# Moving the second pair of state copies of a chunked recurrence from VectorE to ScalarE

## The chip, the cores and the metric

The kernel runs on one core of a Trainium2 chip. A core has a matrix engine (TensorE, in the profile PE, with its weight loads as PEld), VectorE (DVE), ScalarE (ACT), GpSimd (POOL) and a queue for transfers (SyncE, SP). Each works through its own list of instructions in order, and they wait for one another by semaphores. The metric is the device time of one execution in microseconds (us); lower is better.

## The reference

The computation has two stages. The first is a linear recurrence over 768 steps with a 40 x 40 state for each of 4 x 8 = 32 heads. The second is a small mixture of four attention experts on its result.

```python
for t in range(S):                                   # 768 steps, 32 heads, D = 40
    y[:, :, t] = np.einsum('bhd,bhde->bhe', rt, state)
    Sa = np.einsum('bhde,bhe->bhd', state, at)
    state_decay = state * wt[:, :, None, :] - np.einsum('bhd,bhe->bhde', Sa, bt)
    state = state_decay + np.einsum('bhd,bhe->bhde', vt, kt)
x = y of all heads side by side                      # 4 x 768 x 320
for e in range(4):                                   # causal attention of each expert, top 2 of 4 mixed
    a = softmax(causal(scale * (x @ wq[e]) @ (x @ wk[e]).T))
    out += (mask of the top 2) * gate[e] * (a @ (x @ wv[e]) @ wo[e])
```

The change lies in the first stage alone.

## The kernel before

**How the recurrence is tiled.** The 768 steps are cut into 24 chunks of 32 steps, and four chunks make a window (six windows). Within a chunk the steps are written as matrix products: the decays are folded into scaled copies of k, b and a, a triangular 32 x 32 system for each head and chunk is inverted, and the chunk's outputs and the next state come out of a few products. The 32 heads go in four groups of eight, and one group in one chunk is a *unit*: 96 units, numbered `u = 4 * chunk + group`.

**The seven parts of a unit.** `unit(u)` gives them by letters:

- `k` (L358): PE turns the scaled keys (L361); ScalarE copies them into `LS`, rows 0 to 63 (L365).
- `g` (L366): PE multiplies with the group's matrix `GL` (L371); ScalarE copies the result into `GT` (L372).
- `u` (L373): PE applies the inverted system `TT` (L377); ScalarE writes the result into `R` (L378).
- `v` (L379): PE turns `R` (L383); ScalarE copies it into `VU` (L384).
- `f` (L385): PE multiplies with `RB` (L388); VectorE masks the result into `R` (L389).
- `y` (L390): PE multiplies `LS` with `R` into `py` (L396), which holds the output and the new state. The state goes into the next chunk's `R1` (in the profile also `R`) by ScalarE (L406), or in the last chunk of a window, with a factor, by VectorE (L404). The output goes into `XT` by VectorE (L408).
- `t` (L415): PE turns the new state of two units, sixteen heads (L420), into the one tile `PT`, and two copies put it into the next chunk's `LS`, rows 64 to 103. These two copies are the lines of the change. `t` runs for every second unit: for group 0 (heads 0 to 15) and for group 2 (heads 16 to 31), so twice a chunk and 23 times each. In the kernel before, the pair of group 0 is ScalarE's (L427) and the pair of group 2 VectorE's (L425).

**The order.** The order of instructions is written out by hand. The main loop (L511) goes through steps `n`, and in each through the parts in the order of `MAIN` (L433), each for a unit some steps back:

`u` of unit n-1, `g` of n, `y` of n-3, `f` of n-2, `t` of n-6 (even n only), `k`, `v` of n-1.

So between the turnings of `t` in step n and the product `y` that reads their copies PE has `v` of step n, `u` and `g` of step n+1. For group 2, `t` falls on steps with n divisible by 4, for group 0 two steps before.

**The side work.** Into the slots behind these parts the tables `SIDE`, `SIDE1`, `SIDE2` put the preparation of the next window: `prep` (two scans on VectorE at L267 and L273, products at L276 and L281 on VectorE or GpSimd, flags `JK` on ScalarE at L264, copies on ScalarE at L283, the 32 matmuls of `m` and `n` at L289 with VectorE's mask at L290), and `invert` (chains of products and sums at L319 and L321 on VectorE and GpSimd). The sixth window has nothing to prepare, and in its place the second stage's weights are made ready. Side work stands in the same queues as the units' parts, in the order in which it was written.

**The PSUM ring.** `u`, `g`, `f`, `k`, `v`, `m` and `n` share four PSUM buffers `ps`; `PT` has one buffer, and `py` two.

Of the kernel before, what the change touches and what calls it, by code (L numbers as in the profile page):

```python
# [8 lines left out]
AF = mybir.ActivationFunctionType  # L9
# [132 lines left out]
def recurrence(tc, ctx, I, xT, FL, CM, early, tail=None, KP=(11, 11, 11, 11, 11, 11)):  # L142
# [5 lines left out]
    V, A, T, PL = nc.vector, nc.scalar, nc.tensor, nc.gpsimd  # L148

    def ps(shape):  # L150
        return pp.tile(shape, F32, name="ps", tag="ps", bufs=4)
# [198 lines left out]
    def unit(u):  # L350
        c, g = divmod(u, 4)
        w, cw = divmod(c, 4)
        i = w * NG + g
        h0 = 8 * g
        gl, tt, ls, r1, r2, rb, sc = GF[w % 2], TF[w % 2], LS[c % 2], R1[c % 2], R2[c % 2], RB[c % 2], SC[i % 12]
        gt, vu, xt, py = GT[g], VU[u % 2], XT[g // 2][:, 4 * (g % 2):4 * (g % 2) + 4], PY[u % 2]
        rn, ln = R1[(c + 1) % 2], LS[(c + 1) % 2]
        def s_k():  # L358
            p_k = ps([128, 4, 128])
            for p in range(4):  # L360
                T.transpose(p_k[:, p, 0:104], KB[i % NKB][0:104, p * 4 + cw:p * 4 + cw + 2, :].rearrange("q c k -> q (c k)"),  # L361
                            ident[0:104, 0:104])
            p_k = p_k.rearrange("q p (s e) -> q (p s) e", s=2)[:, :, 0:40]
            for k in range(2):
                A.activation((ls, ln)[k][0:64, h0:h0 + 8], p_k[64 * k:64 * k + 64], AF.Copy)  # L365
        def s_g():  # L366
            p_g = ps([33, 8, 40])
            for h in range(8):
                o = 1024 * g + 64 * ((h // 2) * 4 + cw) + 32 * (h % 2)
                r = 104 * ((h0 + h) // 2) + 64 * (h % 2)  # L370
                T.matmul(p_g[:, h], gl[:, o:o + 33], r1[:, r:r + 40], start=True, stop=True)  # L371
            A.activation(gt[32 * g:32 * g + 32], p_g[0:32], AF.Copy)  # L372
        def s_u():  # L373
            p_u = ps([33, 8, 40])
            for h in range(8):
                o = 64 * ((h // 2) * 4 + cw) + 32 * (h % 2)
                T.matmul(p_u[:, h], tt[:, o:o + 33], gt[:, h, :], start=True, stop=True)  # L377
            A.activation(hd(r2[32:64, 40 * h0:40 * h0 + 320], 40), p_u[0:32], AF.Copy, scale=-1.0)  # L378
        def s_v():  # L379
            p_t = ps([80, 4, 66])  # L380
            for p in range(4):
                o = 40 * (h0 + 2 * p)
                T.transpose(p_t[:, p], r2[0:66, o:o + 80], ident[0:66, 0:66])  # L383
            A.activation(vu[0:80], p_t[:, :, 0:64], AF.Copy)  # L384
        def s_f():  # L385
            p_f = ps([64, 8, 32])
            for p in range(4):
                T.matmul(p_f[:, 2 * p:2 * p + 2], vu[:, p, :], rb[:, 4 * g + p, :], start=True, stop=True)  # L388
            V.tensor_tensor(hd(r2[0:64, 1280 + 32 * h0:1536 + 32 * h0], 32), p_f, mask[:, None, :].to_broadcast([64, 8, 32]), op=OP.mult)  # L389
        def s_y():  # L390
            a = r2[:, 0:40]
            for p in range(4):
                for s in range(2):
                    h = h0 + 2 * p + s
                    m = bass.AP(a.tensor, a.offset + 40 * h, [a.ap[0], [1280 - 8 * h, 2], [1, 40]])
                    T.matmul(py[64 * s:64 * s + 40, p], ls[:, h, :], m, start=True, stop=True, tile_position=(0, 64 * s))  # L396
            for s in range(2):
                q = slice(64 * s, 64 * s + 40)
                if c < 23:
                    o = rn[64:104, 52 * h0:52 * h0 + 416].rearrange("q (p e) -> q p e", p=4)[:, :, 64 * s:64 * s + 40]  # L400
                    st = py[q, :, 0]
                    if cw == 3:
                        pn = PC[((c + 1) // 4 * NG + g) % 12]
                        V.tensor_tensor(o, st, pn[q, :, None].to_broadcast([40, 4, 40]), op=OP.mult)  # L404
                    else:
                        A.activation(o, st, AF.Copy)  # L406
            def decay():
                V.tensor_tensor(xt[:, :, 32 * cw:32 * cw + 32], py[0:104, :, 1, 0:32],  # L408
                                sc.rearrange("q (p c) t -> q p c t", p=4)[:, :, cw, 0:32], op=OP.mult)
                if cw == 3:  # L410
                    for s in range(2):
                        nc.sync.dma_start(xT.rearrange("b (p s e) t -> b s e p t", s=2, e=40)[g, s, :, :, 128 * w:128 * w + 128],
                                          xt[64 * s:64 * s + 40])
            return decay
        def s_t():  # L415
            if c == 23:
                return
            for P in range(8):
                o = 52 * h0 + 104 * P
                T.transpose(PT[0:104, P // 4, 104 * (P % 4):104 * (P % 4) + 104], rn[0:104, o:o + 104], ident[0:104, 0:104])  # L420
            for s in range(2):
                o = ln[64:104, h0 + s:h0 + 16:2].rearrange("q (b p) e -> q b p e", b=2)
                x = PT[64 * s:64 * s + 40, :, 0:416].rearrange("q b (p e) -> q b p e", p=4)[:, :, :, 64:104]
                if g:
                    V.tensor_copy(o, x)  # L425
                else:
                    A.activation(o, x, AF.Copy)  # L427
        return dict(k=s_k, g=s_g, u=s_u, v=s_v, f=s_f, y=s_y, t=s_t)


# [80 lines left out]
    for n in range(NU + 4):  # L511
# [4 lines left out]
        for s, (x, d) in enumerate(MAIN):  # L516
            if x == "k":
                g = {7: 0, 1: 1, 3: 2, 5: 3}.get(n % 8)
# [440 lines left out]
```

## Time and profile before

| what | value |
|---|---|
| time, median of 3 runs | 735.41 us (730.02 to 738.67) |
| the profiled execution | 737.55 us, its span 735.5 us |
| PE / PEld / VectorE / ScalarE / GpSimd busy | 636.8 / 563.0 / 519.7 / 466.6 / 333.5 us |
| mean granted clock of TensorE | 0.919 |
| first and last copy of L425 | 112.4 to 480.2 us |
| L425 | 46 copies, 490 ns each at the median |
| L427 | 46 copies, 430 ns each at the median |

The recurrence's steps fill about 80 to 482 us of the span, the second stage the rest. A row of waits says who stood still, on which line, until which other engine's instruction had ended: total, number of times, longest. In the timeline a row is a run of like instructions with its start, its length and, in brackets, the idle time just before it and what ended that. In windows a row is a stretch with the busy time of each engine, the clock that TensorE was granted, the busy share of the DMA engines and what they moved.

### The profile page before, as it was taken

The page shows a single profiled execution, that of the slowest core. Times are in us where ns is not written, and L with a number is a line of the kernel's source. Part 1 is how long each engine was busy: PE and PEld are TensorE (multiplying, and loading weights), DVE is VectorE, ACT ScalarE, POOL GpSimd, SP SyncE. Part 2 cuts the span into 40 slices and gives each one's busy share as a digit, 9 for nine tenths or more (in the row PEclk, how much of TensorE's full clock was granted, in tenths as well). Part 3 has the DMA queues.
Part 4 walks back from the last instruction along what each step waited for, and adds up shares of the span by engine and source line. Part 5 has one row for each costly group of instructions (what it writes and reads, how often), then busy time and mean ns, then how long its engine had stood idle before and what let it go on. Part 6 is the DMA issues. An engine that isn't in the chain of part 4 may idle for free.

```text
span 735.5 us, 22110 instructions
## 1 busy us (share of the span) xinstructions
PE 636.8 (87%) x8801; PEld 563.0 (77%) x8801; DVE 519.7 (71%) x1270; ACT 466.6 (63%) x1144; POOL 333.5 (45%) x512
## 2 busy tenths in 40 slices
PE   5531798898899888988899999979989999999996
PEld 4531788897789777987798999978868777887774
DVE  8899879668866876677657435258797687658651
ACT  6695487477657755766566768727656565656752
POOL 5475388139704850486018301013565354433641
PEclk8555799999999989989999999999999999999999
DMA  7851653575357535753452382143123113201101
GB/s 201 201 149 37 133 159 107 121 199 137 97 136 190 129 89 124 199 130 96 112 147 70 96 227 72 34 140 98 44 69 96 36 39 86 62 28 45 37 32 45
DMA packets 88551, 78.13 MB, mean 106 GB/s; under 512 B 54776, under 2 KB 72952, under 8 KB 88440
## 3 DMA queue, kind: packets, MB, share of 16 engines
q1 hardware_dynamic: 88296, 76.54, 39.9%
q8 instruction: 71, 1.16, 0.7%
q14 instruction: 40, 0.33, 0.2%
q10 hardware_dynamic: 144, 0.10, 0.1%
HBM read 56.17 MB, written 14.16 MB: 96 GB/s over the span
## 4 chain that ended last, share of the span: by engine, by line
PE 59%; DVE 22%; ACT 8%; issue 3%; DMA 1%; SPq 0%; POOL 0%; ACTq 0%; DVEq 0%; POOLq 0%
PE py L396 7%; PE ps L377 6%; PE ot L843 5%; PE ps L289 5%; PE ps L371 5%; PE ps L388 5%; PE sc L795 4%; PE pt L420 4%; PE pt L825 3%; PE pt L852 3%; PE pt L717 3%; PE ps L361 3%; PE pt L736 3%; DVE SC L273 2%; DVE MT L321 2%
## 5 line engine op out<-in xcount | busy, mean ns | idle before, releaser
L817 POOL TENSOR_TENSOR P<-P,m 128x128 f32<-128x128 f32 (+2 forms) x96 | 87.6, 934 | 103.1 <-DVE m L813 50.3
L396 PE MATMUL py<-R,LS 128*40 128x80 f32 x1536 | 84.9, 244 | 31.2 <-DVE LS L425 28.8
L289 PE MATMUL ps<-AB,KB 104*64 104x64 f32 x768 | 68.4, 262 | 38.6 <-ACT LS L365 16.1
L321 POOL TENSOR_TENSOR MT<-MT,TP 128x84 f32<-128x84 f32 (+13 forms) x169 | 89.9, 532 | 13.2
L289 PEld LDWEIGHTS ps<-AB,KB 104*64 104x64 f32 x768 | 63.3, 174 | 42.5 <-ACT LS L365 16.3
L389 DVE TENSOR_TENSOR R<-ps,CM 64x256 f32<-64x256 f32 x96 | 39.9, 415 | 78.4 <-PE ps L388 77.3
L396 PEld LDWEIGHTS py<-R,LS 128*40 128x40 f32 x1536 | 63.7, 122 | 36.3 <-DVE LS L425 33.8
L806 ACT ACTIVATE P<-sc,m 128x128 f32<-128x128 f32 (+2 forms) x96 | 60.7, 633 | 30.2 <-DVE m L805 24.5
L805 DVE TENSOR_REDUCE m<-sc 128x1 f32<-128x128 f32 (+2 forms) x96 | 59.4, 622 | 27.9 <-PE sc L798 26.8
L377 PE MATMUL ps<-GT,TT 128*33 128x40 f32 x1536 | 76.1, 207 | 0.0
L406 ACT ACTIVATE R<-py 40x160 f32<-40x160 f32 x144 | 42.5, 295 | 46.0 <-PE py L396 42.3
L377 PEld LDWEIGHTS ps<-GT,TT 128*33 128x33 f32 x1536 | 65.0, 116 | 7.5 <-issue 1.0
L795 PE MATMUL sc<-ks,qs 128*128 128x384 f32 (+4 forms) x256 | 64.4, 353 | 3.9 <-ACT P L806 3.6
L388 PE MATMUL ps<-RB,VU 128*64 128x64 f32 x768 | 63.4, 228 | 2.1 <-ACT VU L384 2.1
L365 ACT ACTIVATE LS<-ps 64x320 f32<-64x320 f32 x96 | 41.4, 431 | 30.6 <-PE ps L361 29.4
L388 PEld LDWEIGHTS ps<-RB,VU 128*64 128x64 f32 x768 | 56.1, 144 | 3.5 <-ACT VU L384 3.5
L825 PE MATMUL pt<-CM,P 128*128 128x128 f32 x336 | 51.9, 276 | 2.1 <-ACT pt L831 1.7
L319 POOL TENSOR_TENSOR TP<-LT,MT 128x220 f32<-128x220 f32 (+9 forms) x100 | 49.7, 497 | 7.8
L384 ACT ACTIVATE VU<-ps 80x256 f32<-80x256 f32 x96 | 36.4, 379 | 26.3 <-PE ps L383 24.5
L372 ACT ACTIVATE GT<-ps 32x320 f32<-32x320 f32 x96 | 40.7, 424 | 14.8 <-PE ps L371 11.4
L795 PEld LDWEIGHTS sc<-ks,qs 128*128 128x128 f32 x256 | 41.3, 191 | 11.2 <-ACT P L806 8.5
L378 ACT ACTIVATE R<-ps 32x320 f32<-32x320 f32 x96 | 40.9, 426 | 7.6 <-PE ps L377 5.6
(148 smaller groups left out, 1498.0 us busy)
## 6 DMA issues: line engine op xcount, KB each, us to landing
RB<-in_RB SPq DMA_DIRECT2D x24, 320.0 KB
EK<-in_EK SPq DMA_DIRECT2D x18, 416.0 KB
ks<-ks SPq DMA_DIRECT2D x32, 192.0 KB
R<-in_VG SPq DMA_DIRECT2D x24, 208.0 KB
EW<-in_EA SPq DMA_DIRECT2D x18, 214.5 KB
R<-in_VT SPq DMA_DIRECT2D x48, 80.0 KB
R<-in_RT SPq DMA_DIRECT2D x24, 160.0 KB
xT<-XT SPq DMA_DIRECT2D x48, 80.0 KB
```

Source lines behind the costliest of these rows:

```text
L289: T.matmul(p_a[:, p, cc, :], kb[0:104, n, :], AB[0:104, n, :], start=True, stop=True)
L319: return [lambda: e.tensor_tensor(tmp, row[:, None, :].to_broadcast([128, m, n]), M[:, r0:r0 + m, j][:, :, None].to_broadcast([128, m, n]) ...
L321: lambda: e.tensor_tensor(o, o, tmp, op=OP.add)]
L377: T.matmul(p_u[:, h], tt[:, o:o + 33], gt[:, h, :], start=True, stop=True)
L388: T.matmul(p_f[:, 2 * p:2 * p + 2], vu[:, p, :], rb[:, 4 * g + p, :], start=True, stop=True)
L396: T.matmul(py[64 * s:64 * s + 40, p], ls[:, h, :], m, start=True, stop=True, tile_position=(0, 64 * s))
L406: A.activation(o, st, AF.Copy)
L795: T.matmul(ps[:, c, 0:cw], QS[b][:, e, o], KS[b][:, e, z, k], start=(z == 0), stop=(z == 1 and not last), skip_group_check=True)
L805: V.tensor_reduce(m[:, 0, t:t + 1], ps[:, 0:ch, 0:cw], axis=AX.XY, op=OP.max, negate=True)
L806: later(DE, lambda: A.activation(pv, ps[:, 0:ch, 0:cw], AF.Exp, bias=m[:, 0, t:t + 1], accum_out=m[:, 1, t:t + 1]))
L817: PL.tensor_tensor(P[:, 0:n], P[:, 0:n], m[:, 3, t:t + 1].to_broadcast([128, n]), op=OP.mult)
L825: T.transpose(p[:, 128 * y:128 * y + 128], st["P"][t][:, 128 * c:128 * c + 128], ident)
```

## The change

The branch on the group falls away, and both pairs of copies are ScalarE's. The same data go from the same place to the same place, as before; the line numbers behind it fall by three, so that the copies of both groups now stand on L424.

```diff
             for s in range(2):
                 o = ln[64:104, h0 + s:h0 + 16:2].rearrange("q (b p) e -> q b p e", b=2)
                 x = PT[64 * s:64 * s + 40, :, 0:416].rearrange("q b (p e) -> q b p e", p=4)[:, :, :, 64:104]
-                if g:
-                    V.tensor_copy(o, x)
-                else:
-                    A.activation(o, x, AF.Copy)
+                A.activation(o, x, AF.Copy)
         return dict(k=s_k, g=s_g, u=s_u, v=s_v, f=s_f, y=s_y, t=s_t)
```

The instructions of VectorE around the ninth of its 23 pairs, in the third window (`SC` is the scan's result, `AB` the scaled a, `TP` and `MT` the inversion; - stands before and not now):

```order
 L273 SCALAR_TENSOR_TENSOR SC_97<-EW_83,D1P_86 104x528
 L276 TENSOR_TENSOR AB_112<-EA_84,SC_97 40x16x32
-L425 COPY LS_123<-pt 40x8x40 x2
 L319 TENSOR_TENSOR TP_119<-MT_117 128x99
 L321 TENSOR_TENSOR MT_117<-MT_117,TP_119 128x9x11
```

The pair stood behind a scan and a product of the preparation; it goes, and nothing else moves.

The instructions of ScalarE at the same place (`VU`, `GT` and `R` are the unit's own tiles, `JK` the flag; + stands now and not before):

```order
 L372 ACTIVATE GT_134<-ps 32x320
 L406 ACTIVATE R_124<-py_79 40x4x40 x2
+L424 ACTIVATE LS_123<-pt 40x8x40 x2
 L384 ACTIVATE VU_129<-ps 80x256
 L264 ACTIVATE JK,FL<-EW_83,CM 104x512
```

The pair now stands between the copies of `y` and the copy of `v`, the place that the pair of group 0 has two steps earlier. PE, GpSimd and the transfer queue keep their instructions and their order.

## The prediction

> **What bounds the kernel now.** I read the page first, then the waits of the stretch in which the edited line runs, then that line's own rows, the timeline around one copy, and the windows between copies. Busy times show no engine that is full:
>
> ```profile
> span 735.5 us, 22110 instructions
> PE 636.8 (87%) x8801; PEld 563.0 (77%) x8801; DVE 519.7 (71%) x1270; ACT 466.6 (63%) x1144; POOL 333.5 (45%) x512
> ```
>
> So the recurrence is set by who waits for whom. The view of waits between 100 and 482 us has (total us, times, longest us):
>
> ```profile
> DVE R L389 <- PE ps L388: 74.8, 57, 2.8
> ACT R L406 <- PE py L396: 40.3, 16, 4.4
> PE py L396 <- DVE LS L425: 28.8, 25, 3.2
> ACT LS L427 <- PE pt L420: 14.1, 19, 1.2
> PE ps L371 <- ACT VU L384: 2.2, 3, 1.1
> PE ps L388 <- ACT VU L384: 1.6, 7, 0.3
> ```
>
> Of what PE waits for, 28.8 us is for VectorE's copy at L425, and no row names L427, ScalarE's copy of the same shape, as a thing waited for. The two take (ns, least/median/most):
>
> ```profile
> L425 DVE COPY LS<-pt x46: 483/490/496, 112.4 to 480.2; 40x320 f32<-40x320 f32 x46
> L427 ACT ACTIVATE LS<-pt x46: 428/430/433, 102.8 to 474.7; 40x320 f32<-40x320 f32 x46
> ```
>
> The timeline around the ninth of the 23 VectorE pairs shows why PE waits (start us, length us; in brackets the idle time before it):
>
> ```profile
> 253.76 0.92 PE L420 MATMUL pt<-CM,R 104*104 104x104 f32 x8
> ...
> 256.46 0.41 ACT L372 ACTIVATE GT<-ps 32x320 f32<-32x320 f32 x1
> 256.81 1.25 DVE L273 TENSOR_TENSOR_SCAN SC<-EW,D1P 104x528 f32<-104x528 f32 x1
> 258.09 0.75 DVE L276 TENSOR_TENSOR AB<-EA,SC 40x512 f32<-40x512 f32 x1
> 258.87 1.01 DVE L425 COPY LS<-pt 40x320 f32<-40x320 f32 x2
> 259.41 1.68 PE L396 MATMUL py<-R,LS 128*40 128x80 f32 x15 [3.23 <-DVE LS L425]
> ...
> 261.26 0.62 ACT L406 ACTIVATE R<-py 40x160 f32<-40x160 f32 x2 [4.40 <-PE py L396]
> ...
> 261.86 0.42 DVE L389 TENSOR_TENSOR R<-ps,CM 64x256 f32<-64x256 f32 x1 [1.04 <-PE ps L388]
> ```
>
> The turnings that the pair reads end at 253.76 + 0.92 = 254.7, but the copies start at 258.87, behind VectorE's preparation of the next window (a scan of 1.25, a product of 0.75). PE stands 3.23 us before L396, and ScalarE 4.40 us behind PE. The bound here is not a busy engine but a short copy in a long queue.
>
> **The change part by part.** I cut the trace at the starts of VectorE's pairs; the first row holds one pair, the 35.60, 38.10 and 37.80 rows two each, the last eight (stretch; length, busy time and count of PE, weight loads, DVE, ACT, POOL; granted clock, DMA share, GB/s):
>
> ```profile
> 112.40:129.90 17.50, 15.08 (x264) 13.84 (x264) 15.84 (x38) 11.40 (x30) 15.30 (x29) 0.90 0.36 100
> 129.90:152.70 22.80, 21.65 (x360) 20.25 (x360) 14.75 (x36) 13.27 (x30) 2.25 (x6) 0.93 0.61 136
> 167.70:203.30 35.60, 28.46 (x528) 26.04 (x528) 31.32 (x65) 23.18 (x62) 29.25 (x53) 0.95 0.41 110
> 203.30:224.20 20.90, 20.29 (x344) 19.07 (x344) 13.77 (x34) 12.75 (x29) 0.00 (x0) 0.92 0.59 136
> 224.20:240.20 16.00, 15.18 (x315) 14.35 (x313) 11.32 (x25) 11.90 (x29) 9.19 (x14) 1.00 0.77 204
> 240.20:278.30 38.10, 30.95 (x528) 28.30 (x528) 30.52 (x66) 23.18 (x62) 27.55 (x51) 0.87 0.39 107
> 278.30:299.20 20.90, 20.32 (x344) 19.09 (x344) 13.51 (x32) 12.75 (x29) 0.00 (x0) 0.92 0.60 131
> 315.60:353.40 37.80, 31.27 (x528) 28.87 (x528) 29.52 (x66) 23.29 (x62) 26.73 (x49) 0.86 0.36 98
> 353.40:373.20 19.80, 19.19 (x327) 18.04 (x328) 11.05 (x29) 11.12 (x25) 0.00 (x0) 0.91 0.52 117
> 389.90:480.00 90.10, 88.34 (x1796) 83.29 (x1796) 41.83 (x114) 64.81 (x169) 23.02 (x56) 1.00 0.37 99
> ```
>
> PE's wait for L425 in these stretches, in the same order without the 224.20 one, which has none:
>
> ```profile
> PE py L396 <- DVE LS L425: 1.7, 2, 1.5
> PE py L396 <- DVE LS L425: 2.2, 2, 2.0
> PE py L396 <- DVE LS L425: 4.1, 4, 2.4
> PE py L396 <- DVE LS L425: 2.8, 1, 2.8
> PE py L396 <- DVE LS L425: 4.8, 3, 3.2
> PE py L396 <- DVE LS L425: 2.8, 1, 2.8
> PE py L396 <- DVE LS L425: 5.0, 4, 2.9
> PE py L396 <- DVE LS L425: 2.8, 1, 2.8
> PE py L396 <- DVE LS L425: 2.0, 5, 0.9
> ```
>
> They sum to 28.2 us. Removed from VectorE: 46 copies of 0.49, a pair 1.01 as the timeline has it, 23.2 us in all. Added to ScalarE: 46 of 0.43, 19.8 us in all, each pair in the place that the matching pair of L427 has two steps earlier. There ScalarE's copies already cost PE no wait, so I count PE's wait for this copy as gone: **28.2 us**, the first term.
>
> What is late next. At the ninth pair VectorE would have finished its last job ahead of L389 1.01 us sooner, and it idled 1.04 us before L389, so L389 can come 2.05 us earlier at once, not 3.23. The rest has to come out of VectorE's idle time in the following steps. For the seven pairs of the 17.50, 35.60, 38.10 and 37.80 rows VectorE's idle time is 1.66 + 4.28 + 7.58 + 8.28 = 21.8, and the removed pairs add 7.1; neighbours on VectorE stand 0.03 us apart (256.81 + 1.25 to 258.09), about 1 us in a stretch of 32 instructions, 7 in all, which cannot be had. That caps these seven at 22 us. Their waits are 15.6, so the cap lies above the first term, but not far. In the four stretches with the matmuls of the next window (22.80, 20.90 twice, 19.80) VectorE idles 7 to 9 us and PE is busy 19 to 22, so their waits, 10.6, come back whole.
>
> A second gain is possible on top. The stretches that open with a wait show a granted clock of 0.86 to 0.95, the 16.00 one without a wait 1.00. Length times (1 - clock) over the eight low rows is 1.75 + 1.60 + 1.78 + 1.67 + 4.95 + 1.67 + 5.29 + 1.78 = 20.5 us of PE time at full clock. If the waits cause the low clock, the first seven pairs reach their cap of 22, the four others 10.6 + 6.7 = 17.3, and with the last row's 2.0 the gain is 41: the upper end. [...]
>
> The lower end is what VectorE is relieved of where it is late: 13 pairs are waited for over 0.5 us (one in each of the first two rows, two in each long row, one in each of the three that follow these, two in the last), 13 x 1.01 = 13 us. Between 13 and 41 I take 28.2, the waits themselves, the only row that is a measured wait of the engine that sets the pace; it stands in the middle.
>
> The new wait. ScalarE runs in order: behind the pair stand VU (L384), in some steps the flag JK (L264), then R (L378), GT (L372) and L406; PE's next turnings wait for R, its next products for GT and VU. At the ninth pair ScalarE would start it at 254.7, end the rest 0.89 later than now, at 256.87 + 0.89 = 257.8, and still idle over 3 us of the 4.40 if L396 did not move. When L396 moves up to 259.41 - 3.23 = 256.2, right behind the matmuls before it, ScalarE is about 1 us late for L406, and part of the gain passes through it. That is inside my caps. For the ten pairs that PE does not wait for by over 0.5 us, the price is between 0 and 10 x 0.89 = 8.9 us; in the last row PE is busy 88.34 of 90.10 and ScalarE 64.81, which its eight pairs raise to 72, so I take **1 us**.
>
> [...]
>
> The sum: the profiled execution took 737.55, its span of 735.5 and 2.05 around it. 737.55 - 28.2 + 1 = 710.4. The median of the runs shown, 735.41, lies 2.1 lower, which gives 708.2. I say 709.
>
> **The rivals.**
>
> *VectorE's queue was the bound, and the copy only showed it.* PE runs ahead and then waits for R from L389, which stands behind the same scans. Then a waited pair brings only 1.01 us: 737.55 - 13 + 1 = 725.5. For it: in the 35.60 row VectorE is busy 31.32. Against: L389 itself waits for PE 74.8 us, in 57 places. 12%. In its extreme form PE's wait just changes its name and the time stays at 737: 8%.
>
> *The clock comes back too.* 737.55 - 41 = 696.5. For it: low clock only behind waits. Against: the last row has waits and a clock of 1.00, so not every wait lowers it. 12%. [...]
>
> *ScalarE becomes the bound, and the kernel is slower.* If each pair's 0.89 us lands on the path through VU, R and GT, 23 x 0.89 = 20.5 are added, and PE's 28.2 reappear as waits on ScalarE: 737.55 + 20.5 = 758. It decides where ScalarE's idle time in a step falls under 0.89 us. For it: PE already waits for VU in ten places, 3.8 us in all, and ScalarE's 40.3 us before L406 exist only because PE is late. Against: in the 38.10 row ScalarE is busy 23.18, and its two pairs more, 1.8 us, still fit. 8%.
>
> **How the numbers follow.** Forecast 60% (702 to 718), VectorE's queue 12% (725), name change 8% (737), clock 12% (697), ScalarE 8% (758). From 697 to 727 the forecast, the first rival and more than half of the clock's are held, 8 in 10. About 1% is what a measurement of this kernel can tell from no change, 728 and 743 here. Faster: 60 + 12 + 9 = 81%; same: 8 and a part of the 725 case, 11%; slower 8%.
>
> **What would show it.** Right: no wait of PE for the copy; PE's other waits up by less than 5 us; ScalarE's idle time before L406 down from 40.3 to under 20; the plain stretches at 15.5 to 17.5 us each instead of 17.5 to 19; the granted clock above 0.95 between 112 and 373 if the clock follows. Wrong: a new row of 10 us or more in which PE waits for R of L389 (VectorE's queue) or for VU, R or GT (ScalarE), or longer stretches in the last 90 us.

## The result and the profile after

The changed kernel takes 703.12 us (median of 4 runs, 702.29 to 706.51), the kernel before beside it 736.95 (4 runs). The ratio is 0.957, with a 95% interval of 0.949 to 0.964; forecast were 709 us and a range of 697 to 727. A second set of runs gave 706.13 against 735.55, ratio 0.960 (0.955 to 0.965). The profiled execution took 706.51, 31.0 less than the one before.

The page of the changed kernel, span and busy times:

```profile
span 704.4 us, 22098 instructions
PE 618.0 (88%) x8801; PEld 547.4 (78%) x8801; DVE 496.1 (70%) x1224; ACT 486.4 (69%) x1190; POOL 342.6 (49%) x512
```

VectorE has lost 23.6 us of work and ScalarE gained 19.8, about what the 46 copies take on each. PE is busy 18.8 us less with the same 8801 matmuls, so its matmuls became faster, not fewer (mean granted clock 0.945, before 0.919).

The waits of the changed kernel between 100 and 450 us (total us, times, longest us):

```profile
DVE R L389 <- PE ps L388: 63.1, 40, 2.8
ACT LS L424 <- PE pt L420: 27.6, 37, 1.6
PE ps L371 <- DVE R L389: 4.9, 4, 1.7
PE ps L289 <- DVE R L389: 3.7, 3, 1.5
PE ps L371 <- ACT VU L384: 3.5, 5, 0.8
PE ps L371 <- ACT LS L365: 1.5, 3, 0.6
PE ps L377 <- DVE GLe L290: 1.4, 1, 1.4
ACT R L406 <- PE py L396: 0.9, 2, 0.7
PE ps L388 <- ACT VU L384: 0.9, 4, 0.3
PE py L396 <- ACT LS L424: 0.3, 1, 0.3
```

PE's 28.8 us for the copy are gone but for 0.3. ScalarE's idle time ahead of L406 fell from 40.3 to 0.9, which shows that it was PE's lateness passed on. In return PE now waits 8.6 us in seven places (the third and fourth rows) for VectorE's mask L389, which before it did not.

The ninth pair of group 2 in the timeline of the changed kernel, rows of PE, ScalarE and VectorE in order of time:

```profile
240.46 0.92 PE L420 MATMUL pt<-CM,R 104*104 104x104 f32 x8
241.42 0.89 ACT L424 ACTIVATE LS<-pt 40x320 f32<-40x320 f32 x2 [0.63 <-PE pt L420]
242.33 0.38 ACT L384 ACTIVATE VU<-ps 80x256 f32<-80x256 f32 x1
242.71 0.72 PE L396 MATMUL py<-R,LS 128*40 128x80 f32 x15
243.80 1.25 DVE L273 TENSOR_TENSOR_SCAN SC<-EW,D1P 104x528 f32<-104x528 f32 x1
245.08 0.79 DVE L276 TENSOR_TENSOR AB<-EA,SC 40x512 f32<-40x512 f32 x1
245.79 0.25 DVE L319 TENSOR_TENSOR TP<-MT 128x99 f32<-128x99 f32 x1
246.07 0.45 DVE L321 TENSOR_TENSOR MT<-MT,TP 128x99 f32<-128x99 f32 x1
246.44 0.41 DVE L389 TENSOR_TENSOR R<-ps,CM 64x256 f32<-64x256 f32 x1
246.99 0.76 PE L371 MATMUL ps<-R,GLe 128*33 128x40 f32 x15 [1.66 <-DVE R L389]
247.62 1.27 PE L396 MATMUL py<-R,LS 128*40 128x80 f32 x15
```

The copies start 0.96 us after the turnings' start (before: 5.11), and L396 starts without a wait. Four microseconds later PE meets the same scan and product again: L389 stands behind them, and L371 waits 1.66 us for L389 to have read its `ps` buffer. From the turnings of this pair to those of the next it is now 17.1 us, and was 19.85.

Two windows, of the kernel before and of the changed one, from the first to the last turnings of group 2 (length; busy time and count of PE, weight loads, DVE, ACT, POOL; clock, DMA share, GB/s):

```profile
109.00:479.00 370.00, 338.08 (x6306) 315.85 (x6304) 247.21 (x578) 243.78 (x616) 161.76 (x303) 0.94 0.49 126
```

```profile
108.70:448.00 339.30, 322.68 (x6302) 303.83 (x6302) 224.50 (x534) 262.53 (x660) 172.07 (x304) 0.98 0.54 137
```

The stretch is 30.7 us shorter. PE's busy time accounts for 15.4 of them, at a clock of 0.98 instead of 0.94; the time in which PE was not busy accounts for as much (370.00 - 338.08 = 31.9 before, 339.30 - 322.68 = 16.6 now), and the waits that the views name fit it (28.8 + 2.2 + 1.6 = 32.6 before, 16.2 in the rows above).

### The profile page after: what moved, and what is told of

The parts are those of the page before. It is cut to its first block, busy times and chain, and to the rows that moved or that the text cites. A ratio compares the mean times of both kernels' runs of the same rounds, so it can differ in the third digit from the quotient of the medians.

```text
span 704.4 us, 22098 instructions
## 1 busy us (share of the span) xinstructions
PE 618.0 (88%) x8801; PEld 547.4 (78%) x8801; DVE 496.1 (70%) x1224; ACT 486.4 (69%) x1190; POOL 342.6 (49%) x512
## 4 chain that ended last, share of the span: by engine, by line
PE 53%; DVE 30%; DMA 7%; ACT 6%; issue 3%; SPq 1%; POOL 0%; DVEq 0%; ACTq 0%; POOLq 0%
PE ps L377 5%; PE py L396 5%; PE ot L840 5%; PE ps L371 5%; DVE MT L321 5%; PE ps L289 4%; PE sc L792 4%; DVE TP L319 4%; PE ps L388 4%; PE pt L714 4%; PE pt L420 3%; PE pt L822 3%; PE pt L849 3%; DVE SC L273 3%; DVE AB L276 3%
## 5 line engine op out<-in xcount | busy, mean ns | idle before, releaser
L289 PE MATMUL ps<-AB,KB 104*64 104x64 f32 x768 | 63.8, 251 | 44.4 <-ACT LS L365 16.9
L321 POOL TENSOR_TENSOR MT<-MT,TP 128x84 f32<-128x84 f32 (+13 forms) x169 | 92.1, 545 | 13.2
L289 PEld LDWEIGHTS ps<-AB,KB 104*64 104x64 f32 x768 | 58.6, 163 | 48.4 <-ACT LS L365 17.1
L389 DVE TENSOR_TENSOR R<-ps,CM 64x256 f32<-64x256 f32 x96 | 39.6, 413 | 68.7 <-PE ps L388 67.9
L396 PE MATMUL py<-R,LS 128*40 128x80 f32 x1536 | 77.5, 237 | 3.3 <-DVE R L389 2.3
L396 PEld LDWEIGHTS py<-R,LS 128*40 128x40 f32 x1536 | 59.5, 119 | 4.2 <-DVE R L389 2.4
L388 PE MATMUL ps<-RB,VU 128*64 128x64 f32 x768 | 61.3, 224 | 1.5 <-ACT VU L384 1.4
L424 ACT ACTIVATE LS<-pt 40x320 f32<-40x320 f32 x92 | 39.6, 431 | 28.9 <-PE pt L420 27.6
L319 POOL TENSOR_TENSOR TP<-LT,MT 128x220 f32<-128x220 f32 (+9 forms) x100 | 54.9, 549 | 7.8
L388 PEld LDWEIGHTS ps<-RB,VU 128*64 128x64 f32 x768 | 53.9, 139 | 3.1 <-ACT VU L384 3.1
L406 ACT ACTIVATE R<-py 40x160 f32<-40x160 f32 x144 | 42.7, 297 | 6.8 <-PE py L396 2.9
L828 ACT ACTIVATE pt<-pt 128x512 f32<-128x512 f32 (+1 forms) x64 | 34.4, 542 | 17.4 <-PE pt L822 16.6
```

The source lines that it names most:

```text
L289: T.matmul(p_a[:, p, cc, :], kb[0:104, n, :], AB[0:104, n, :], start=True, stop=True)
L319: return [lambda: e.tensor_tensor(tmp, row[:, None, :].to_broadcast([128, m, n]), M[:, r0:r0 + m, j][:, :, None].to_broadcast([128, m, n]) ...
L321: lambda: e.tensor_tensor(o, o, tmp, op=OP.add)]
```

## The experiments

Two theories stood at the start. *Queue*: a pair costs where it is late in VectorE's queue, by the wait of PE. *Load*: the gain is VectorE's relief of 23 us, wherever it falls. A third, *clock*, came from the two windows: the waits lower the granted clock, and that is about half of the gain. All times are medians beside runs of the kernel before on the same chip.

| run | time | ratio to before (95%) |
|---|---|---|
| changed kernel, first and second set | 703.1, 706.1 | 0.957 (0.949 to 0.964), 0.960 (0.955 to 0.965) |
| only the 13 waited pairs moved | 704.9 | 0.959 (0.952 to 0.966) |
| only the other ten moved | 736.7 | 1.000 (0.997 to 1.004) |
| copies stay VectorE's, ahead of the side work | 719.1 | 0.976 (0.969 to 0.982) |
| before, wait filled with 43 us of matmuls | 732.0 | 0.995 (0.992 to 0.999) |
| before, wait filled with 21 us | 723.2 | 0.982 (0.979 to 0.984) |
| changed, each copy twice | 714.5 | 0.971 (0.967 to 0.976) |
| changed, idle work on VectorE instead of the copies | 721.9 | 0.980 (0.976 to 0.983) |
| changed, eight products to GpSimd | 734.2 | 0.996 (0.992 to 0.999) |
| all 92 copies on VectorE | 750.2 | 1.017 (1.013 to 1.021) |
| changed, end of the inversion behind f | 700.2 | 0.951 (0.946 to 0.956) |
| the same, two more inversion steps moved | 702.6 | 0.955 (0.950 to 0.960) |

**Which pairs pay.** The thirteen, and the ten, against the kernel before:

```diff
-                if g:
+                if g and c not in (0, 1, 3, 4, 5, 7, 8, 9, 11, 12, 13, 15, 16):
                     V.tensor_copy(o, x)
```

```diff
-                if g:
+                if g and c in (0, 1, 3, 4, 5, 7, 8, 9, 11, 12, 13, 15, 16):
                     V.tensor_copy(o, x)
```

> Only the 13 pairs of group 2 that TensorE visibly waited for are moved to ScalarE (chunks 0, 1, 3, 4, 5, 7, 8, 9, 11, 12, 13, 15, 16); the other ten stay VectorE's. Theory Q (a pair costs where it is late in VectorE's queue): the whole gain, within 2 us of the changed kernel, about 703. Rival L (the gain is VectorE's load, 23 us less): 13/23 of 33.8, about 718.

> The complement: only the ten pairs that TensorE did not wait for are moved to ScalarE. Theory Q: no gain, 735 to 738, and no loss either, since ScalarE has room. Rival L: 10/23 of 33.8 less, about 722. Rival S (ScalarE's time is on the path there): 10 x 0.89 more, up to 746.

The thirteen alone brought the whole gain, 0.959; the other ten nothing, and cost nothing either. A row of PE's waits in the run with the ten shows that the wait stayed where it was:

```profile
PE py L396 <- DVE LS L425: 28.5, 24, 3.5
```

A general relief of VectorE is thereby out: 9.8 us less of its time in the ten places changed nothing. So is a price of ScalarE's in those places.

**Same engine, other place in the queue.** The copies stay VectorE's, and in their steps the side work between f and t is written behind them:

```diff
-            for f in jobs.get((n, s), []):
-                f()
+            if not (n % 4 == 0 and s == 3):
+                for f in (jobs.get((n, 3), []) if n % 4 == 0 and s == 4 else []) + jobs.get((n, s), []):
+                    f()
```

> All 46 copies of group 2 stay VectorE's, as before, but in their steps they stand ahead of the side work that was written between f and t, and no longer behind it. Theory Q: TensorE's wait for them falls from 28.8 to under 5 us and the time to 703 to 712, with VectorE as loaded as before. Rival L: as before, 735 to 738. If the side work is then late for the next mask: something between, with new waits for L389.

719.1 us, a little over half of the gain. PE's waits in this run, 100 to 482 us:

```profile
PE ps L289 <- DVE R L389: 5.6, 2, 2.8
PE py L396 <- DVE LS L425: 3.1, 11, 0.8
PE py L396 <- DVE R L389: 2.8, 3, 1.2
PE ps L371 <- DVE R L389: 2.3, 2, 1.5
PE ps L377 <- DVE R L389: 1.2, 1, 1.2
```

The wait for the copy is down from 28.8 to 3.1 with VectorE as loaded as before: the place in the queue is a cause by itself. But 11.9 us of waits for L389 stand in its stead, since the scans that were pushed back are now late for the mask.

**VectorE's load without a wait for it.** To the changed kernel, where each pair stood on VectorE, come two reductions of a constant whose result nobody uses:

```diff
                 A.activation(o, x, AF.Copy)
+                if g:
+                    z = CM[64:104, None, 0:160].to_broadcast([40, 2, 160])
+                    V.tensor_reduce(SCR[64:104], z, axis=AX.X, op=OP.max)
```

> The changed kernel with two small reductions of a constant (40 x 320, about 0.4 to 0.5 us each, result unused) on VectorE where each pair of copies stood: VectorE is as busy as before the change, but nobody waits for that work. If only PE's wait for the copy mattered: 703 to 706. If half of the gain is VectorE's relief of about 1 us at the 13 late pairs (as the run with the copies ahead of the side work suggests): 713 to 720, with more waits of PE for L389.

721.9 us: 2.0 to 2.3% of the time before, 14 to 17 us, are lost again, though each reduction takes only what a copy took and has no reader. Its duration in the view by line (its first and last start in us, 46 of them), and PE's waits for L389, which stands at L390 in this kernel:

```profile
L428 DVE TENSOR_REDUCE SCR<-CM x46: 482/482/484, 111.5 to 467.8; 40x2 f32<-40x320 f32 x46
```

```profile
PE ps L372 <- DVE R L390: 10.0, 4, 3.1
PE ps L290 <- DVE R L390: 7.5, 3, 2.6
```

The waits for L389 double, from 8.6 to 17.5. Both runs come to about the same state by different ways: VectorE is loaded as before and PE hardly waits for the copy, and about half of the gain is there. So the change does two things, and each is worth about half: the copy leaves the place behind the scans, and what stands behind the copy, L389, comes a microsecond earlier where VectorE is late.

**The clock.** To the kernel before, ahead of y in the 13 waited steps, come matmuls on constants into the columns that y overwrites, so that the wait stays and PE is busy in it. The first try put in 620:

```diff
             a = r2[:, 0:40]
+            for k in range({0: 34, 1: 49, 3: 33, 4: 58, 5: 63, 7: 34, 8: 72, 9: 63, 11: 42, 12: 69, 13: 63, 15: 24, 16: 16}.get(c - 1, 0) if g == 2 else 0):
+                T.matmul(py[64 * (k % 2):64 * (k % 2) + 40, 0], CM[:, 0:40], CM[:, 0:80], start=True, stop=True, tile_position=(0, 64 * (k % 2)))
```

> The kernel before, with 16 to 72 extra matmuls on constants ahead of y in the 13 waited steps, into the py columns that y overwrites (37 ns each, sized under the wait), so that TensorE is busy through most of the wait while the wait itself stays. Theory C (the waits lower the granted clock, and the clock is about half of the gain): clock 0.98 or more between 112 and 390 us instead of 0.86 to 0.95, time 720 to 729. Rival (the low clock has another cause): clock as before, time 735 to 740.

This was sized wrongly. A row of its timeline at the ninth pair (a matmul leaves two records, 1240 for the 620 over the run):

```profile
254.21 5.15 PE L392 MATMUL py<-CM 128*40 128x80 f32 x143
```

The 72 matmuls took about 5 us, 69 ns each, where the wait was 3.23; they pushed y back themselves. The clock over 112 to 390 us rose to 1.00, but the time says nothing of what that is worth. So the same with half the numbers (17, 24, 16, 29, 31, 17, 36, 31, 21, 34, 31, 10, 6):

> The run with the filled wait again, with half the filling: there each matmul took two passes, 69 ns and not 37, so that the filling (43 us in all) was longer than the wait (28) and pushed y back. Here 6 to 36 matmuls, 21 us in all, which end before the copy does. Theory C (a clock that stays up is worth something by itself, though VectorE's queue is as before): clock 0.98 or more between 112 and 390 us, time 720 to 729. Rival (VectorE sets the pace there, and a faster PE just waits longer): clock up all the same, time 730 to 736, and PE's wait for L425 with the filling added at 28 us or more.

723.2 us, 1.9% faster than before (0.979 to 0.984), with not a copy moved. The window from 112 to 390 us of the kernel before and then of this run, and PE's wait for the copy (L425 stands at L427 here):

```profile
112.00:390.00 278.00, 248.13 (x4472) 231.06 (x4472) 203.25 (x460) 177.12 (x443) 136.08 (x245) 0.93 0.53 134
112.00:390.00 278.00, 264.21 (x5312) 246.72 (x5308) 214.09 (x486) 186.21 (x468) 152.63 (x266) 1.00 0.54 137
```

```profile
PE py L398 <- DVE LS L427: 7.5, 25, 0.9
```

PE stands still or multiplies constants for about 7.5 + 21 = 28 us, as long as it waited before, and the clock over the window is 1.00, where the kernel before had 0.93. The waits do lower the clock, and the low clock by itself cost 14 us.

The trace of the kernel before shows it right behind the waits. At the ninth pair, the 3 us of the wait and the nine that follow:

```profile
256.41:259.41 3.00, 0.00 (x0) 0.00 (x0) 2.90 (x5) 0.46 (x2) 2.77 (x4) 0.82 0.07 19
259.41:262.41 3.00, 2.96 (x28) 2.56 (x29) 1.89 (x6) 0.59 (x2) 2.53 (x7) 0.50 0.18 64
262.41:265.41 3.00, 3.00 (x46) 2.84 (x46) 2.80 (x8) 1.68 (x5) 2.53 (x7) 0.54 0.00 0
265.41:268.41 3.00, 3.00 (x63) 2.85 (x58) 2.11 (x7) 2.09 (x6) 2.45 (x8) 1.00 0.62 177
```

The clock is halved for some six microseconds behind the wait and then whole again; the fifteen matmul records of L396 take 1.68 us there and 0.72 in the changed kernel. Ten of the thirteen waits, 1.35 to 3.23 us long, are followed by such a fall, to between 0.50 and 0.83 in the next 3 us; the other three, 1.28, 0.89 and 0.54 us long, leave it at 1.00.

**ScalarE's room.** In the changed kernel each copy of group 2 is done twice:

```diff
                 A.activation(o, x, AF.Copy)
+                if g:
+                    A.activation(o, x, AF.Copy)
```

> The changed kernel with each copy of group 2 done twice on ScalarE: 46 copies, 19.8 us, more in the same places. If ScalarE hides its share (the two-way move showed no loss for ten pairs): up to 4 us slower than the changed kernel, 703 to 707. If ScalarE is by now the bound: 23 x 0.89 = 20.5 more, about 724.

714.5 us, 8 to 11 more than the changed kernel, between the two expectations. PE's waits have a new row (the second copy stands at L426):

```profile
PE py L396 <- ACT LS L426: 6.1, 19, 0.7
```

In the last 90 us too, where PE before the change was busy for 88.34 of 90.10 us, a stretch from one pair's turnings to the next grew from 12.79 to 13.25 us. There one pair of 0.89 us hides in a step, and two do not.

**All on VectorE.** The branch goes the other way, both groups to VectorE:

> Both groups' pairs on VectorE: 46 more copies there, 22.5 us. Theory: where scans and products stand ahead of group 0's pairs as well, PE waits for them too, 2.2 us in each late pair; with 10 to 13 late ones and their load, 755 to 775. Rival (the two groups differ, only group 2's place is late): 740 to 748.

750.2 us, under the expected 755 to 775 and over the rival's 748. PE's wait grew by a third only, not to double:

```profile
PE py L396 <- DVE LS L425: 38.2, 42, 2.8
```

Group 0's place is late too, but less so; VectorE's further 22.5 us of load were not separated from that.

**A product to GpSimd.** Four entries of the tables give eight of VectorE's products L276 to GpSimd, among them:

```diff
-    -12: "///1s t1 1x t1///1f",
+    -12: "///1s t1 1X t1///1f",
```

> The changed kernel with eight of VectorE's products of the preparation (0.75 to 0.9 us each, behind the scan at -12 and -8 in the tables of the third window on) given to GpSimd. If what is left is VectorE's queue ahead of L389 (PE waits 9.3 us for it): 697 to 701. If GpSimd's slower product (1.57 us) delays the inversion or the flags behind it: no gain, 703 to 706, or slower.

A miss: 734.2 us, the gain is gone. Rows of its waits:

```profile
PE ps L289 <- DVE R L389: 13.0, 3, 5.5
PE ps L383 <- DVE R L389: 10.8, 1, 10.8
DVE KB L281 <- DMA EK<-in_EK: 24.2, 6, 12.8
```

VectorE waits for the load of the next `EK` in six places, 24.2 us in all; in the changed kernel it was 2.3 us in three places, in the kernel before none. The product reads the single buffer `EA`. The longest of the six waits in the timeline (rows of GpSimd, the transfer queue and VectorE):

```profile
128.63 1.17 POOL L276 TENSOR_TENSOR AB<-EA,SC 40x512 f32<-40x512 f32 x1
129.83 0.31 SPq L206 DMA_DIRECT2D EA<-in_EA  x1
131.45 0.33 SPq L206 DMA_DIRECT2D EK<-in_EK  x1
139.47 0.69 DVE L281 TENSOR_TENSOR KB<-EK,SUF 104x512 f32<-104x512 f32 x1 [12.76 <-DMA EK<-in_EK]
```

The product stands in GpSimd's queue behind that engine's part of the inversion and ends at 129.80. The next load of `EA` is issued 0.03 us later, that of `EK` behind it in the queue at 131.45, and VectorE stands 12.76 us until 139.47. In the changed kernel the same two loads were issued at 115.71 and 119.02, and the same product of `EK` had no wait. I had counted GpSimd's time for the product and not the buffer that it holds, nor the queue behind that. The other five waits are 0.83 to 3.48 us long, and they need not all have this cause: at the one of 3.48 us, `EK` was issued at 273.72, only 0.35 us after VectorE itself had finished reading that buffer.

**What is left.** The rest of a window's inversion on VectorE (token S) goes behind f of its step:

```diff
-    -3: "/S//3X/0m//0nodq",
+    -3: "///S 3X/0m//0nodq",
-    -3: "/S 3Xw//0n/0m//0qo 3l",
+    -3: "/3Xw//S 0n/0m//0qo 3l",
```

> The changed kernel with the last eight or so inversion instructions of a window on VectorE (the token S at -3 of two tables) written behind f of their step and no longer ahead of it, so that the mask L389 no longer stands behind them. If VectorE's queue ahead of L389 is what is left: PE's wait of L289 for L389 (3.7 us in three places) goes and the time falls 3 to 6 us, to 697 to 700. Rival (GpSimd or the store of the inverse behind S is what ends last there): 703 to 707.

700.2 us beside 706.1 for the changed kernel in the same set (

> The changed kernel once more beside these two, on the same chip: 702 to 707.

), 5.9 less; the intervals of the two ratios touch (0.946 to 0.956 and 0.955 to 0.965), but all four runs of the one (699.1 to 700.6) lie below all four of the other (704.5 to 706.5). The row in which L289 waits for L389 is gone from PE's waits; this one stays:

```profile
PE ps L371 <- DVE R L389: 4.4, 4, 1.5
```

The second edit moved two inversion steps on in one table (-12 to `"///1s 1x///1f"`, -10 to `"///1y t4/t3//1ve"`):

> As e9, and two inversion instructions each moved from -12 (behind the scan and ahead of the late L389 of that step) two rows on in the table of the fourth to sixth windows. If VectorE's queue ahead of L389 at these places (4.9 us of PE's wait in four places) is what is left: 2 to 4 us below e9. Rival (VectorE is full over the whole stretch there): the same as e9.

702.6 us, no better than without it. L371's wait for L389 falls from 4.4 to 0.9, and a wait for ScalarE's copy L378 takes its place:

```profile
PE ps L371 <- ACT R L378: 6.4, 4, 2.1
```

## Why the prediction was right, and where its working was not

The forecast of 709 and "faster" held, the measured 703 lies 6 lower, and the mechanism was in part the one named: PE waited for a short copy behind VectorE's side work, and on ScalarE that wait is gone. That the number came so close is luck, as the terms show. They are given here by the length from one pair's turnings (L420, group 2) to the next in both timelines:

| term | forecast | measured |
|---|---|---|
| seven pairs in the plain stretches | 15.6, capped at 22 | 16.94, 15.89, 18.23, 16.8, 19.85, 18.04, 18.7 to 15.22, 14.95, 14.97, 14.35, 17.1, 14.46, 15.41: 18.0 |
| four with the next window's matmuls | 10.6, with the clock 17.3 | 24.52, 23.39, 23.43, 23.42 to 23.25, 20.11, 21.87, 19.68: 9.9 |
| the two late ones | 2.0 | 14.26, 13.91 to 12.79, 12.78: 2.6 |
| ten unwaited pairs, ScalarE's price | 1 (0 to 8.9) | 0.0; the nine stretches that such a pair opens are within 0.01 |

**The first term, 28.2 us, had the right size for the wrong reason.** I counted PE's wait for the copy as gone and took nothing for the clock. The wait did go, but 12 us came back under other names, 8.6 of them L389; that is 16 us net. The other half of the gain is the clock, 15.4 us of PE's busy time. The two errors cancelled, by luck. The step that failed is "I take 28.2, the waits themselves": it should have been the waits less what VectorE's queue holds back, plus the clock.

**VectorE's queue was treated as a rival (12%) and was a part of the sum.** The rival said that PE would meet the same scans at L389; at the ninth pair it does, 1.66 us long. The lower end of 13 us, VectorE's relief at the late pairs, is close to what the run with idle work on VectorE gave back (14 to 17), but that relief is paid on top of the earlier copy, not in its place.

**The clock.** The 20.5 us of PE time that I set as its upper bound were the right thing to look at, and I gave them 12%. Against them I had the last 90 us, with waits and a clock of 1.00; the two longest there, 0.89 and 0.54 us, are two of the three behind which the clock stays at 1.00. No single wait exceeds 3.23 us, and eight of the thirteen longer ones are 1.5 to 3; filled with matmuls, the same waits leave the clock at 1.00 instead of 0.93 and the kernel 14 us faster. So it is the waits that lower the clock in the kernel before: the fall, to between 0.50 and 0.83 in the next 3 us, stands right behind each of ten single waits of 1.35 to 3.23 us.

**The cap on the seven pairs held** (18.0 under 22). The four waits that were to come back whole did so in their sum (9.9 for 10.6) and not one by one: for waits of 2.2, 2.8, 2.8 and 2.8 the stretches gained 1.3, 3.3, 1.6 and 3.7. The two that gained least have a new wait and a low clock in the changed kernel (1.40 us at 131.34 and 1.50 us at 264.17, with a clock of 0.57 over 131 to 135 and over 264 to 268 us). **ScalarE's price** was counted at 1 and is nothing; the room it has was not much more than that, as the doubled copies show. The rival in which ScalarE becomes the bound is out for one pair and begins with the second.

**The signs named ahead.** No wait for the copy: right, 0.3. ScalarE's idle time before L406 under 20: right, 0.9. Clock above 0.95 between 112 and 373: right, 0.98 over the whole recurrence. Plain stretches of 15.5 to 17.5: they went lower, 14.4 to 17.1. PE's other waits up by less than 5: wrong, the rows shown rose from 3.8 to 15.9. The sign against the forecast, a new row of 10 us or more of waits for L389, did not come, but by little: two rows with 8.6 together.

What stays open: how far each of the three parts would go without the other two was measured for one part at a time only (place in the queue 18, clock 14, VectorE's relief 14 to 17, together 29 to 34). They overlap, and no run separates the overlap: from the first to the last turnings, the run with the copies ahead of the side work has 327.7 us of busy PE at a clock of 0.97 and the one with idle work on VectorE 331.3 at 0.95, beside 338.1 at 0.94 before and 322.7 at 0.98 after, so a part of the clock's share lies in each of the two halves.

## What to carry to other kernels

In this kernel a short copy between two products of the pacing engine belonged on the engine whose queue was free when its input arrived (at the ninth pair it starts 0.96 us after the start of the turnings, and started 5.11 us after it in the longer queue), and the shares of busy time (71% and 63%) did not show which that is or at which places it matters; the timeline around one such copy shows the first, and the wait list says at how many places it pays. After such a wait is removed, look for the next instruction that stood behind the copy in the same queue, since that is where PE stopped next here (L389, 8.6 us in seven places). And count short waits of TensorE twice when the granted clock is low behind them: once as the wait, once as the slower matmuls that follow (here the first fifteen records took 1.68 us behind a wait of 3.23 us, at a clock of 0.50, and 0.72 without a wait).

## What the runs showed of the hardware that was not expected

TensorE's granted clock had means of 0.86 to 0.95 over stretches in which it never stood for more than 3.23 us at once: it fell to between 0.50 and 0.83 in the 3 us behind ten waits of 1.35 to 3.23 us, and stayed at 1.00 behind three of 0.54 to 1.28 us. Over 112 to 390 us it was 1.00 instead of 0.93 when 21 us of matmuls on constants filled these waits. Eight products moved to GpSimd cost 31 us (734.2 beside 703.1), where the one in the timeline above takes 1.17: in the longest wait that followed, the late read of a single load buffer held that buffer's next load and the one behind it in the transfer queue, and VectorE stood 12.8 us for the second.
